# Two-bank PSUM tiles read behind both products, another stage order, and weight sums spread over two chunks, in a fused attention and mixture kernel

## The chip, the cores and the metric

One core of one Trainium2 chip; each call of experiments ran on another chip, with the kernel before beside it. The metric is the device time of one execution in microseconds (us). Each time is a median over repeated executions; profiles show one execution each, and their span is about 2 us shorter than the time of the same run. The interval behind a ratio is its 95% interval.

Engines in the listings: PE does matmuls, PEld loads their weights, DVE is the vector engine, ACT the scalar engine, POOL is GpSimd, SP issues DMAs. PSUM is the memory into which PE writes its products; a tile of it spans two banks in this program, and to evict a result is to read it out of PSUM. The granted clock is PE's clock as the trace records it, 1.00 being full speed. L751 is line 751 of the kernel. In a kernel with another number of lines the same statement may have another number; where it matters, it is said.

## The reference, cut to what matters

```python
# attention over sorted blocks: 4 batches x 8 heads x 768 tokens x 64
P = sinkhorn(sort_net)                       # 8x8 mixing matrices, five rounds
k_sorted, v_sorted = P mixed with k, v       # per head, over 8 blocks of 96 tokens
attn = softmax(scale * q_b @ k_sorted_b.T);  x = attn @ v_sorted_b
# mixture of four experts on the 3072 x 512 result
p = domain_probs / domain_probs.sum(-1)
for e in range(4):
    h = maximum(x @ w1[e], 0)                # w1: 512 x 1024
    out += p[:, e:e+1] * (h @ w2[e])         # w2: 1024 x 512
```

## The kernel before

Everything runs in one program with a hand-made order. The 3072 tokens are worked on in twelve chunks of 256, three to a batch (in the text chunks count from 1, in the code `c` counts from 0). A chunk has hidden-layer groups (16 matmuls each, evicted by DVE in L772) and then second-layer products by a scheme with seven products and sums of operands. The first six chunks (batches 0 and 1) also carry, in numbered slots between their groups and products, the pieces of the next batch's attention: `st_n` and `st_q` load and transpose queries, `st_k` and `st_v` mix keys and values, `st_s` are scores, `st_a` attention, `st_x` the transposed result. The last six chunks use the seven-product scheme on both layers; the change does not touch them.

The slots and who calls them:

```python
def slot(b=b, c=c, at=at):
    here = (c, at[0])                        # chunk, number of the slot
    for cc, n, f, *args in PLANS[b]:         # attention of the next batches
        if (cc, n) == here: f(*args)
    if b:
        for cc, n, e, m in PLAN_A:           # sums of w1 blocks, on DVE, L961
            if (cc, n) == here: input_sums(e, m)
    ...                                      # cut
    at[0] += 1
```

The products of a chunk of batch 0 (c > 0); four banks in two PSUM tiles:

```python
two = [psm([P, 2, 512], F32, ...) for n in range(2)]
bankA, bankB, bankC, bankQ = [two[n // 2][:, n % 2, 0:DH] for n in range(4)]
...                                          # cut
times(bankA, blk(0, 0), "b11", es)           # 12 matmuls of 256 columns (L751)
tt(oa1, bankA, oa1, ALU.add)                 # L855, DVE reads bank A
slot()
times(bankB, blk(1, 0), "b21", es)           # the other bank of the same tile
tt(oa1, bankB, oa1, ALU.add)                 # L858
slot()
...                                          # cut: bank C, bank Q
times(bankA, sm(1), "t2", es, False)         # next writer of the first tile
```

In batch 1 the four experts make 16 matmuls, and instead of L855 ACT copies bank A away (L826) between the two products.

The softmax here doesn't subtract the row's maximum and nothing guards it: scores larger than these inputs give would overflow.

Of the kernel before, what the change touches and what calls it, by code (L numbers as in the profile page):

```python
# [12 lines left out]
ALU = mybir.AluOpType  # L13
# [4 lines left out]
def kernel(  # L18
# [11 lines left out]
    nc = tc.nc  # L30
# [180 lines left out]
    def load_p(b, c):  # L211
        pb = moe.tile([P, E, 2 * P], F32, name=f"pb_{b}_{c}", tag="pb", bufs=1)
        nc.sync.dma_start(
            pb[:],
            p_dram[:, ds(b * S + 2 * c * P, 2 * P)].rearrange("(o e) x -> o e x", o=1).broadcast_to([P, E, 2 * P]),
        )
        return pb
# [380 lines left out]
    def st_bk(b, qd):  # L598
# [4 lines left out]
    PLANS = {  # L603
        0: [
            (0, 9, st_v, 1, 0), (0, 10, st_q, 1, 0), (0, 10, st_v, 1, 1), (0, 11, st_k, 1, 0), (0, 11, st_n, 1, 1),
            (1, 0, st_q, 1, 1), (1, 0, st_k, 1, 1), (1, 0, st_n, 1, 2), (1, 1, st_v, 1, 2), (1, 2, st_s, 1, 0),
            (1, 3, st_v, 1, 3), (1, 3, st_q, 1, 2), (1, 4, st_s, 1, 1), (1, 4, st_n, 1, 3), (1, 5, st_a, 1, 0),
            (1, 6, st_x, 1, 0), (1, 7, st_k, 1, 2), (1, 7, st_lv, 2, 0), (1, 9, st_a, 1, 1), (1, 9, st_q, 1, 3),
            (1, 9, st_lv, 2, 1), (1, 10, st_x, 1, 1),
            (1, 11, st_s, 1, 2), (1, 12, st_lk, 2, 0),  # L610
            (2, 0, st_a, 1, 2), (2, 0, st_n, 2, 0), (2, 0, st_n, 2, 1), (2, 0, st_n, 2, 2), (2, 0, st_n, 2, 3),
# [133 lines left out]
    def times(ps, lhs, rhs, es, first=True, done=True, between=None, at=None):  # L745

        for e in es:
            if e == at:
                between()
            for f in range(KH):  # L750
                nc.tensor.matmul(  # L751
                    ps, lhs(e, f), Ts[e][rhs][:, f, :],
                    start=(first and e == es[0] and f == 0), stop=(done and e == es[-1] and f == KH - 1),
                    skip_group_check=True,
                )
# [25 lines left out]
    def chunk(b, c, slot, done=()):  # L781

        es = list(range(E)) if b else list(range(1, E))
        todo = [e for e in es if e not in done]
        chunk_first(b, c, todo, todo[0], slot)

        for w in range(1, 4 if b else 1 + c if c else 3):
            h_sums(E - 1, w)
        nxt = (b, c + 1) if c + 1 < R // 2 else (b + 1, 0)
        pbs[nxt] = load_p(*nxt)  # L790

        blk = lambda kh, tok: (lambda e, f: Hb[:, e, kh * KH + f, ds(tok * P, P)])
        sm = lambda n: (lambda e, f: Sb[:, n, e, ds(f * P, P)])

        def product(n, lhs, rhs, pool=psm):
            ps = pool([P, DH], F32, f"ps_{n}_{b}_{c}")
            for e in es:
                if pool is last_bank and e == 2:
                    last["e0"][6]()
                for f in range(KH):  # L800
                    nc.tensor.matmul(
                        ps[:], lhs(e, f), Ts[e][rhs][:, f, :],
                        start=(e == es[0] and f == 0), stop=(e == E - 1 and f == KH - 1),
                    )
            return ps[:]

        if b:
            oa, ob = [moeo.tile([P, Dm], F32, name=f"{n}_{b}_{c}", tag="oacc") for n in ("oa", "ob")]
        else:
            oa, ob = oaccs[2 * c], oaccs[2 * c + 1]  # L810
        p1, p5, u2, u3 = [moe.tile([P, DH], F32, name=f"{n}_{b}_{c}", tag=n, bufs=1) for n in ("p1", "p5", "u2", "u3")]
        tt, gtt = nc.vector.tensor_tensor, nc.gpsimd.tensor_tensor
        o = out[ds(b * S, S), :].rearrange("(t p) d -> p t d", p=P)
        oa1, oa2, ob1, ob2 = oa[:, 0:DH], oa[:, DH:Dm], ob[:, 0:DH], ob[:, DH:Dm]

        def store(n, tile):
            nc.sync.dma_start(o[:, 2 * c + n, :], tile[:])

        if b or c:
            two = [psm([P, 2, 512], F32, f"ps_p{n}_{b}_{c}") for n in range(2)]  # L820
            bankA, bankB, bankC, bankQ = [two[n // 2][:, n % 2, 0:DH] for n in range(4)]
            if last:
                bankQ = last["Q"][1][:, 0:DH]
        if b:
            times(bankA, blk(0, 0), "b11", es)
            nc.scalar.copy(p1[:], bankA)  # L826
            slot()
            times(bankB, blk(1, 0), "b21", es)
            tt(oa1, bankB, p1[:], ALU.add)
            slot()  # L830
            times(bankQ, sm(0), "t1", es)
            nc.scalar.copy(p5[:], bankQ)
            slot()
            for e in es:
                h_sums(e, 4)
            times(bankA, sm(1), "t2", es, False)
            nc.scalar.copy(u2[:], bankA)
            slot()
            times(bankC, blk(1, 1), "n4", es)
            nc.scalar.copy(ob1, bankC)  # L840
            slot()
            times(bankA, sm(2), "t3", es, False)
            tt(ob2, bankA, p5[:], ALU.add)
            tt(ob1, bankA, ob1, ALU.add)
            store(1, ob)
            slot()
            times(bankQ, sm(3), "b22", es, False, True, last["e0"][6] if last else None, 2 if last else None)
            tt(oa2, bankQ, u2[:], ALU.add)
            slot()
            store(0, oa)  # L850
            return
        if c:
            both = ob.rearrange("p (h d) -> p h d", h=2)
            times(bankA, blk(0, 0), "b11", es)
            tt(oa1, bankA, oa1, ALU.add)  # L855
            slot()
            times(bankB, blk(1, 0), "b21", es)
            tt(oa1, bankB, oa1, ALU.add)  # L858
            slot()
            for w in range(1 + c, 4):  # L860
                h_sums(E - 1, w)
            times(bankC, blk(1, 1), "n4", es[:1], True, False)
            times(bankQ, sm(0), "t1", es)
            tt(ob2, bankQ, ob2, ALU.add)
            slot()
            for e in es:
                h_sums(e, 4)
            times(bankA, sm(1), "t2", es, False)
            tt(oa2, bankA, oa2, ALU.add)
            slot()  # L870
            next(sums0)
            times(bankC, blk(1, 1), "n4", es[1:], False)
            tt(ob1, bankC, ob1, ALU.add)
            slot()
            times(bankA, sm(2), "t3", es, False)
            tt(both, bankA.rearrange("p (o d) -> p o d", o=1).broadcast_to([P, 2, DH]), both, ALU.add)
            slot()
            store(1, ob)
            next(sums0)
            times(bankQ, sm(3), "b22", es, False)  # L880
            tt(oa2, bankQ, oa2, ALU.add)
            slot()
            store(0, oa)
            return

        def f1():
            nc.scalar.copy(p1[:], product("p1", blk(0, 0), "b11", psm if c == 1 else psa))
            slot()
            gtt(oa1, oa1, p1[:], ALU.add)

        def f2():
            tt(oa1, product("p2", blk(1, 0), "b21"), oa1, ALU.add)
            slot()

        def f3():
            tt(oa2, product("p3", sm(3), "b22"), oa2, ALU.add)
            slot()

        def f4():
            tt(ob1, product("p4", blk(1, 1), "n4"), ob1, ALU.add)  # L900
            slot()

        def f5():
            nc.scalar.copy(p5[:], product("p5", sm(0), "t1"))
            slot()
            gtt(oa2, oa2, p5[:], ALU.add)
            gtt(ob2, ob2, p5[:], ALU.add)

        def last_adds(u3):
            gtt(ob2, u3, ob2, ALU.add)  # L910
            tt(ob1, ob1, u3, ALU.add)

        steps = weight_sums(E - 1, nc.vector)
        f1()
        for e in todo:
            h_sums(e, 4)
        next(steps)
        f2()
        next(steps)
        h_sums(E - 1, 3)  # L920
        f3()
        next(steps)
        f5()
        next(steps)
        tt(u3[:], product("p7", sm(2), "t3"), p1[:], ALU.add)
        slot()
        ps6 = product("p6", sm(1), "t2")
        tt(u2[:], ps6, p1[:], ALU.add)
        tt(u3[:], ps6, u3[:], ALU.add)
        slot()  # L930
        gtt(oa2, u2[:], oa2, ALU.add)
        store(0, oa)
        last_adds(u3[:])
        f4()
        store(1, ob)
# [145 lines left out]
    def last_chunk(g):  # L1081
# [85 lines left out]


    PLAN_A = [
        (1, 11, 0, 0), (1, 13, 0, 1), (2, 1, 0, 2), (2, 2, 1, 0), (2, 3, 1, 1), (2, 4, 1, 2), (2, 5, 2, 0),  # L1170
        (2, 8, 0, 3), (2, 9, 2, 1), (2, 9, 1, 3), (2, 10, 2, 2), (2, 11, 2, 3), (2, 13, 3, 0), (2, 13, 3, 1),
    ]
    late_sums = {(G0, 1): [(3, 2)], (G0, 2): [(3, 3)]}

# [164 lines left out]
```

## Time and profile before

| | before |
|---|---|
| time, median of 3 runs | 382.05 us (381.69 to 382.42) |
| span of the profiled run | 379.1 us |
| PE busy | 358.8 us, 95% |
| PE idle, named after the reads of bank A (L855, L826) | 6.3 us in four waits |
| PE idle, before scores | 3.0 us in two larger waits |
| the last section, six chunks on both layers | 156.5 us from its first product (222.57 us), untouched |

How to read it: PE is the bound nearly throughout, so one looks at what ends each of its idle times, and at whether it runs at full clock. The busy share cannot tell the second: a matmul at half clock counts as busy for longer. The prediction below shows the waits and chains. Four rows of PE's timeline carry one thing more (start, us, engine, line, operation, count, idle before and who ended it), from the third chunk of batch 0:

```profile
116.48 1.92 PE L751 MATMUL ps_p<-w,Hb 128*128 128x256 f16 x12 [2.46 <-DVE room L855]
118.19 1.09 PE L438 MATMUL ps_a<-vs,ET 96*128 96x65 f16 x16
119.09 1.04 PE L751 MATMUL ps_p<-T,Hb 128*128 128x256 f16 x4
119.93 1.89 PE L751 MATMUL ps_p<-w,Sb 128*128 128x256 f16 x12
```

Twelve matmuls of 256 columns take 1.47 us in such a row at full clock, and the 16 of attention 0.65. Behind the 2.46 us wait all four rows are stretched: this is the half clock. In the trace it lasts 3.41 us, from about 117.36 us, so it sets in 0.9 us after PE has resumed.

### The profile page before, as it was taken

To read this page: it belongs to the slowest core of one execution; us is meant where nothing else is said; L and a number is where in the kernel's file an instruction comes from. 1 tells how busy PE (TensorE), PEld (TensorE's weight loads), DVE (VectorE), ACT (ScalarE), POOL (GpSimd) and SP (SyncE) were. 2 spreads that over 40 slices of the span, in tenths; PEclk is the share of its full clock that TensorE was granted. 3 is DMA by queue.
4 is the path that set the end of the run, shared out by engine and by line. 5 is a ranking of instruction groups with operands and counts; after the bars stand their busy time and mean duration, and the time that the engine had idled before them with its cause. 6 is when DMAs were issued, how large, how long until landed. Compare 5 with 4: busy or idle time off the path is not lost.

```text
span 379.1 us, 10548 instructions
## 1 busy us (share of the span) xinstructions
PE 358.8 (95%) x4517; PEld 315.1 (83%) x4517; DVE 280.5 (74%) x558; ACT 157.6 (42%) x282; POOL 117.4 (31%) x134
## 2 busy tenths in 40 slices
PE   8699999967997999999999899999999999999996
PEld 8585858856886887878887799899899898998995
DVE  5654798655896677578669969967868679688694
ACT  2674330533130563436530027347165283471750
POOL 8862101931300054000000005508137064081360
PEclk9999999999998999999999999999999999999999
DMA  8999999999954899963941110220210202103101
GB/s 106 208 208 229 208 209 199 183 177 168 208 70 77 141 164 177 110 124 80 119 105 23 56 43 18 42 73 2 58 57 4 87 26 57 58 2 57 57 13 44
DMA packets 69753, 38.34 MB, mean 101 GB/s; under 512 B 40390, under 2 KB 64716, under 8 KB 69708
## 3 DMA queue, kind: packets, MB, share of 16 engines
q0 software_dynamic: 34640, 17.83, 36.6%
q1 hardware_dynamic: 35068, 19.85, 26.1%
q8 instruction: 35, 0.57, 0.6%
q14 instruction: 10, 0.08, 0.1%
HBM read 42.00 MB, written 6.34 MB: 128 GB/s over the span
## 4 chain that ended last, share of the span: by engine, by line
PE 72%; DVE 14%; DMA 7%; ACT 2%; issue 2%; POOL 2%; DVEq 0%; ACTq 0%; POOLq 0%
PE ps_Q L1114 14%; PE ps_p L751 13%; PE ps_h L766 12%; PE ps_X L1025 8%; PE ps_Q L1025 5%; PE ps_Z L1025 5%; DVE Sb L737 4%; DVE Hb L772 3%; DMA arena<-in_v_dram 3%; PE ps_h L659 3%; PE ps_o L694 3%; DMA qT<-arena 2%; DVE Sb L739 2%; DMA arena<-in_q_dram 2%; PE ps_s L406 1%
## 5 line engine op out<-in xcount | busy, mean ns | idle before, releaser
L1038 POOL TENSOR_TENSOR Hb<-tmp,pb 128x512 f16<-128x512 f32 x48 | 61.9, 1295 | 155.4 <-ACT tmp L1037 153.3
L766 PE MATMUL ps_h<-xT,w 128*128 128x256 f16 x672 | 79.3, 273 | 0.9 <-DVE Hb L772 0.7
L766 PEld LDWEIGHTS <-w 128*128 128x128 f16 x672 | 64.4, 98 | 10.4 <-issue 1.6
L772 DVE SCALAR_TENSOR_TENSOR Hb<-ps_h,pb 128x1024 f16<-128x1024 f32 x42 | 51.3, 1221 | 20.9 <-PE ps_h L766 20.8
L1025 PEld LDWEIGHTS <-w 128*128 128x128 f16 x768 | 46.6, 98 | 1.0 <-issue 0.3
L1114 PEld LDWEIGHTS <-Sb 128*128 128x128 f16 x384 | 36.7, 98 | 6.7 <-DVE Sb L737 2.7
L1025 PEld LDWEIGHTS <-arena 128*128 128x128 f16 x576 | 34.7, 98 | 0.2
L1037 ACT ACTIVATE tmp<-tmp 128x512 f32<-128x512 f32 x48 | 30.5, 635 | 6.4 <-DVE tmp L1069 5.2
L396 ACT CAST kT<-ps_k 64x384 f16<-64x384 f32 x48 | 22.7, 473 | 20.8 <-PE ps_k L387 19.8
L751 PEld LDWEIGHTS <-Sb 128*128 128x128 f16 x288 | 27.7, 99 | 3.8
L1114 PEld LDWEIGHTS <-Hb 128*128 128x128 f16 x288 | 27.4, 98 | 2.9
L751 PEld LDWEIGHTS <-Hb 128*128 128x128 f16 x216 | 20.9, 99 | 10.4 <-issue 7.8
L1025 PE MATMUL ps_X<-kT,arena 128*128 128x128 f16 x384 | 29.3, 219 | 0.0
L121 POOL DMA_DIRECT2D arena<-in_q_dram x24 | 19.8, 837 | 23.6 <-DMA qT<-arena 13.4
L1114 PE MATMUL ps_Q<-w,Sb 128*128 128x256 f16 x192 | 25.8, 273 | 1.0 <-DVE Sb L737 1.0
L737 DVE TENSOR_TENSOR Sb<-Hb 128x512 f16<-128x512 f16 x45 | 26.4, 606 | 0.0
L1061 DVE TENSOR_TENSOR tmp<-ps_Q,tmp 128x512 f32<-128x512 f32 x24 | 16.6, 690 | 12.7 <-ACT tmp L1060 8.5
L413 ACT ACTIVATE ET<-ps_s 96x768 f16<-96x768 f32 x24 | 18.0, 802 | 16.1 <-PE ps_s L406 15.9
L751 PE MATMUL ps_p<-w,Hb 128*128 128x256 f16 x144 | 17.8, 277 | 6.7 <-DVE room L855 5.0
L1114 PE MATMUL ps_Q<-w,Hb 128*128 128x256 f16 x192 | 23.9, 273 | 0.0
L1045 ACT COPY ps_X<-ps_Z 128x512 f32<-128x512 f32 x24 | 13.7, 570 | 23.3 <-PE ps_Z L1025 22.7
L1114 PE MATMUL ps_Q<-T,Sb 128*128 128x256 f16 x192 | 22.9, 273 | 0.0
(188 smaller groups left out, 605.6 us busy)
## 6 DMA issues: line engine op xcount, KB each, us to landing
w<-in_moe_w_dram POOLq DMA_DIRECT2D x7, 1024.0 KB, 27.7
pb<-p_dram SPq DMA_DIRECT2D x12, 512.0 KB, 5.8
arena<-in_k_dram POOLq DMA_DIRECT2D x8, 384.0 KB, 7.9
arena<-in_v_dram POOLq DMA_DIRECT2D x8, 384.0 KB, 9.1
vs<-arena SPq DMA_DIRECT2D x36, 66.0 KB, 5.2
arena<-in_q_dram POOLq DMA_DIRECT2D x24, 96.0 KB, 7.4
out_dram<-ob SPq DMA_DIRECT2D x9, 256.0 KB, 2.0
out_dram<-oa SPq DMA_DIRECT2D x8, 256.0 KB, 2.5
```

The lines of the kernel that those rows point to most:

```text
L121: nc.gpsimd.dma_start(t[:, h // 2, :, h % 2, :], q[b, h].rearrange("(t p) d -> p t d", p=P))
L396: nc.scalar.copy(kT[ds(D * hh, D), r], pk[ds(D * r, D), hh].rearrange("p a (i c) -> p a i c", c=CP),)
L413: nc.scalar.activation(ETs[2 * (pr % 2) + hh][:, 0:S].rearrange("c (a x) -> c a x", a=2), pss[hh][0:BLK, :, 0:HS], AF.Exp, bias=0.0, scale ...
L737: tt(sm[0], blk(0, 1), blk(1, 1), ALU.add)
L751: nc.tensor.matmul(ps, lhs(e, f), Ts[e][rhs][:, f, :], start=(first and e == es[0] and f == 0), stop=(done and e == es[-1] and f == KH - 1 ...
L766: nc.tensor.matmul(ps[:, f, :], w1sb[e][:, kc, ds((4 * g + f) * P, P)], xT[:, kc, ds(2 * c * P, 2 * P)], start=(kc == 0), stop=(kc == NKC ...
L772: nc.vector.scalar_tensor_tensor(out=Hb[:, e, ds(4 * g, 4), :], in0=ps[:], scalar=0.0, op0=ALU.max, in1=pb[:, ds(e, 1), :].broadcast_to([P ...
L1025: nc.tensor.matmul(dst[:, ds(f * P, P)], a[lhs][:, k, ds(f * P, P)], t[rhs][:, k, :], start=(first and f == 0 and k == 0), stop=(f == KH - ...
L1037: nc.scalar.activation(src, src, AF.Relu, bias=0.0, scale=1.0)
L1038: nc.gpsimd.tensor_tensor(Hb[:, e, ds(i * KH, KH), ds(j * P, P)], src.rearrange("p (f x) -> p f x", f=KH), pb[:, ds(e, 1), ds(j * P, P)].b ...
L1061: tt(t22, Q, u3, ALU.add)
L1114: nc.tensor.matmul(ps, lhs(e, f), Ts[e][rhs][:, f, :], start=(first and e == 0 and f == 0), stop=(e == E - 1 and f == KH - 1), skip_group_ ...
```

## The change

Its intent: take PE's idle time out of the chunks of batches 0 and 1. It has three parts and adds or removes no arithmetic.

```diff
-  (1,0,st_n,1,2), (1,1,st_v,1,2), (1,2,st_s,1,0), (1,3,st_v,1,3), (1,3,st_q,1,2), (1,4,st_s,1,1), (1,4,st_n,1,3),
-  (1,5,st_a,1,0), (1,6,st_x,1,0), (1,7,st_k,1,2), ...
+  (1,0,st_n,1,2), (1,1,st_s,1,0), (1,2,st_v,1,2), (1,3,st_v,1,3), (1,3,st_q,1,2), (1,3,st_n,1,3), (1,5,st_s,1,1),
+  (1,6,st_a,1,0), (1,7,st_k,1,2), (1,7,st_x,1,0), ...
@@ products of batch 1
             times(bankA, blk(0, 0), "b11", es)
-            nc.scalar.copy(p1[:], bankA)
             slot()
             times(bankB, blk(1, 0), "b21", es)
+            nc.scalar.copy(p1[:], bankA)
             tt(oa1, bankB, p1[:], ALU.add)
@@ products of batch 0
             times(bankA, blk(0, 0), "b11", es)
-            tt(oa1, bankA, oa1, ALU.add)
             slot()
             times(bankB, blk(1, 0), "b21", es)
+            tt(oa1, bankA, oa1, ALU.add)
             tt(oa1, bankB, oa1, ALU.add)
@@ weight sums: (chunk, slot, expert, sum)
-  (1,11,0,0), (1,13,0,1), (2,1,0,2), (2,2,1,0), (2,3,1,1), (2,4,1,2), (2,5,2,0), (2,8,0,3), (2,9,2,1), ...
+  (1,8,0,0), (1,10,0,1), (1,12,0,2), (1,12,1,0), (1,13,1,1), (1,14,1,2), (2,2,2,0), (2,4,2,1), (2,6,2,2), (2,9,0,3), ...
```

## The prediction

> **What bounds the kernel now.** I read the busy shares first, then the tensor engine's waits, then the chain of work that ended last around each wait, and last the timelines of PE, DVE and ACT there.
>
> From the page (engine, busy us, share of the span; then the granted clock in 40 slices of 9.5 us):
>
> ```profile
> PE 358.8 (95%) x4517; PEld 315.1 (83%) x4517; DVE 280.5 (74%) x558; ACT 157.6 (42%) x282; POOL 117.4 (31%) x134
> ...
> PEclk9999999999998999999999999999999999999999
> ```
>
> PE is busy nearly throughout, so only what removes PE's idle time, or PE time at a lower clock, can pay; the change removes no matmul. One slice (114 to 123 us) has a lower clock: the clock record in the trace has a stretch of 3.41 us at half speed from about 116.5 us.
>
> The waits of PE that the change can touch (engine, output, line <- releaser: total us, times, longest):
>
> ```profile
> PE ps_p L751 <- DVE room L855: 5.0, 2, 2.5
> ...
> PE ps_s L406 <- DMA qT<-arena: 1.6, 1, 1.6
> ...
> PE ps_s L406 <- ACT arena L360: 1.4, 1, 1.4
> ...
> PE ps_p L751 <- ACT p L826: 1.3, 2, 0.8
> ```
>
> L855 and L826 read bank A, the first half of a two-bank PSUM tile; the matmuls that wait for them write bank B, the other half. The kernel has five such places (second and third chunk of batch 0, three chunks of batch 1), and in all five B starts only after A's read ends. Nothing in the data asks for that: the wait comes with sharing the tile.
>
> The chain around the first place (start, us, what):
>
> ```profile
> 69.35 6.28 DMA arena<-in_q_dram
> 75.63 0.02 issue
> 75.64 8.92 DMA qT<-arena
> 84.57 0.05 issue
> 84.61 0.51 PE ps_s L406 x16
> 85.13 1.87 PE ps_h L766 x16
> ...
> 87.02 1.23 DVE Hb L772
> ...
> 89.06 0.69 DVE xsl L423
> ...
> 89.89 0.69 DVE xsl L423
> 90.58 0.33 DVE Sb L737
> 90.91 0.34 DVE room L855
> 91.26 0.04 issue
> 91.30 1.47 PE ps_p L751 x12
> ```
>
> The scores of batch 1's second head pair wait for transposed queries, which land at 84.57. After them comes one more group of hidden-layer matmuls (1.75 us), and then B's product stands behind everything DVE has queued ahead of the read of A: the last group's eviction, two normalisations of attention, a sum.
>
> Third, the last chunk of batch 1:
>
> ```profile
> 207.75 1.21 DVE Hb L772
> 208.96 0.33 DVE Sb L739
> 209.29 0.34 DVE Sb L741
> 209.63 0.60 DVE arena L961
> 210.23 1.15 DVE Hb L772
> 211.38 0.04 issue
> 211.42 1.92 PE ps_p L751 x16
> ```
>
> Here DVE sets the pace (17.29 of the 18 us from 194 to 212 are DVE-busy): evictions L772 at about 1.13 us start to start, sums of activations at 0.33, and the weight sums L961 at 0.60 each stand in one queue, and PE's next product waits for the eviction that ends it.
>
> **What the Trainium skill says.** "PSUM — Partial Sum Buffer", section "PSUM bank collisions raise a hardware error", asks for guarding PSUM by bank and quadrant. The trace is stricter: two different banks of one tile are ordered, five times of five. "TensorE: Matmul & The Clock Gate", Part 1, describes a clock halved by an idle activity window of 3413 ns that runs free; the trace agrees in length (3.41 us at 0.5, at a PE wait of 2.46 us), but the wait of 2.52 us at 88.8 brought no such stretch, so the phase matters. "DMA: Bandwidth & Descriptors", "Issuing engines are not separate DMA queues", has all DMAs share 16 engines: the trace agrees, the transpose took 8.9 us from issue at 75.6 and 2.7 us when issued near 122, where the DMAs were less busy. "Perfetto Trace Analysis", "Optimization Strategy", advises judging each regime by itself, as I do.
>
> **The change part by part.** The pieces of attention are called at numbered slots: after each group of hidden-layer matmuls, then after each product. One 128x256 product over three experts is 12 matmuls, 1.31 us start to end of stream; over four experts 16, 1.75 us; an attention product 0.48; scores 0.44; a v or k stage 0.33.
>
> *Other stage order (chunk 2 of batch 0).* The first scores move ahead of the v stage whose ACT cast (L360) waits for earlier stores of v. I follow PE from 72.7: first group to 74.79; scores, half of them held until ACT finishes evicting the k stage at 75.17, so done about 75.65; four more groups and two v stages, then the sixth group ends near 83.3. The second scores now stand after all six groups. But their queries still land at 84.57: those loads and the transpose are issued ahead of all that moves, and the software DMA queue is full either way. So PE waits 1.2 us, scores 84.61 to 85.06, and the former sixth group (1.75 us) is already done. What replaces the old 1.45 and 1.57 us waits is one wait that ends at the same moment; the gain is the group moved in front of it.
>
> *Banks read behind both products, same chunk.* Product A 85.06 to 86.37; attention, with its second half held about 0.05 to 0.1 us until ACT's exponentials end (85.1 + 2x0.75), to 86.9; B at 86.9 in place of 91.30: 4.4 us gained. Now the order behind it: DVE normalises until about 88.4, then reads A and B until 89.1. The next writer of that tile is the t2 product, after a k stage and 16 matmuls, at 90.25, so the delayed reads are hidden. Later the last product waits about 0.3 us for DVE's read of bank C. I keep 4.25 at the chunk's end.
>
> *Same, chunk 3 of batch 0.* A ends at 113.87 and B started at 116.48: 2.6 us. Without this idle time the half-speed stretch should go too: B's 12 matmuls took 1.75 instead of 1.31, attention 0.88 instead of 0.48, the next four 0.84 instead of 0.44, together 1.2 us. Following the rest of the chunk with DVE's queue (reads of A and B at 116.02 to 116.7, normalisation to 118.4, then 0.34 to 0.7 per instruction) gives two new waits of about 0.1 and 0.15 us, and the chunk ends at 123.46 on the old clock of the trace against 127.44: 4.0 us. The last transposed input, issued at 118.45 with 2.8 us to landing (as the one issued at 120.7 has now), is there by 121.3, before 123.46.
>
> *Batch 1, chunks 1 and 2.* In the first, A ends 145.93 and B started 146.84 because ACT's copy stood behind four casts of k: 0.9 us; but the scores two stages on need a buffer that DVE's normalisation frees, which comes only about 0.5 us earlier: 0.65 us kept. In the second, B starts 0.3 us earlier and ACT's copy moves behind the casts, which frees another buffer 0.35 us earlier: 0.35 kept.
>
> *Weight sums over two chunks, and chunk 3 of batch 1.* Six weight sums instead of two lie in chunk 2, where DVE has gaps of 1.7, 1.1, 2.3 and 0.9 us; three fit into them whole, the one in its last slot delays the first eviction of chunk 3 by about 0.4 us, eating the 0.35. Then only two sums instead of five stand ahead of the seventh eviction: 3x0.60 = 1.8 us less on DVE, so it ends at 209.65 instead of 211.36. PE's eight groups, followed against these evictions, end at 209.65 too. A starts at 209.9 (211.42 before), and B follows at once at 211.65 (213.84 before, of which 0.67 was the wait for the copy): 2.2 us. DVE's queue behind it has room, since two sums fewer stand after A as well; I expect the 2.2 to last to the start of the last section (about 153 us, from 227), which the change does not alter.
>
> Sum: 4.25 + 4.0 + 0.65 + 2.2 = 11.1 us. I take off 0.9 for waits I cannot see, mostly the transposed queries of the third head pair: issued about 84.65 with 9.2 us to landing, as now, they arrive at 93.9, and PE wants them at 94.2. 382.05 - 10.2 = 371.8 us.
>
> **The rivals.** (1) *The data is the bound around 100 us.* DMA is at 90% or more until about 104 us, so work moved earlier may only wait for queries or transposed inputs. For: the second scores do exactly this. Against: the third pair's queries had 3 us to spare before (landed 95.5, used 98.76), and their transpose moves forward by 1.6 us. If half the first gain is lost: 374. (2) *DVE takes PE's place.* The reads queue up behind the normalisations and the tile is then late for t2. For: in chunk 3 of batch 0 DVE is 0.75 us behind. Against: 1.75 us of other products lie in between. If t2 waits a microsecond in each of five chunks: 376, within 2%. (3) *ACT's copy now waits for B too*, so DVE's sum of both is late and drags the normalisations. That is already in the 0.65; double it and 0.5 us more is lost. (4) *The half-speed stretch moves and does not go*, since its window runs free: the new 1.2 us wait is shorter than any that brought one, but if so, 1.2 us is lost: 373. (5) Better than expected: if the queries land earlier than 84.57, up to 1.2 us more.
>
> **Range and chances.** Each of the two large terms is tied to starts and ends in the trace to some tenths; downstream waits are likelier to take than to give. 80% range: 369.0 to 375.5. The 2% line is 374.4, so the gain must fall by a quarter to miss it: faster 0.86, within 2% 0.13, slower 0.01.
>
> **What would show it.** The wait of L751 for L855 and for L826 gone; scores of the second pair still released by the query transpose near 84.6, with an idle of about 1.2 us; B about 87; chunk 3 of batch 0 starting its products near 108 and no half-speed stretch there; the last section starting about 10 to 11 us earlier and lasting as long as now. Wrong would be: a wait of L751 for the new reads of A and B ahead of t2, a wait of the third pair's scores for queries of over 1 us, or a DVE-paced last chunk of batch 1 as long as before.

## The result, and the profile after

| | before | after |
|---|---|---|
| time, median, same rounds | 381.87 us (380.89 to 382.42, 4 runs) | 370.75 us (370.15 to 371.02, 4 runs) |
| ratio, 95% interval | | 0.971 (0.969 to 0.973) |
| span of the profiled run | 379.1 us | 368.1 us |

The change is faster by 2.9%. The prediction was 371.8 us.

The page of the changed kernel, busy shares and clock:

```profile
PE 356.6 (97%) x4517; PEld 314.3 (85%) x4517; DVE 280.3 (76%) x558; ACT 157.6 (43%) x282; POOL 117.4 (32%) x134
...
PEclk9999999999999999999999999999999999999999
```

The same matmuls are 2.2 us less busy. Most of it is the slice with the lower clock, which is gone: the first experiment's kernel, with no such slice and the same matmuls, shows 357.2 us.

The chain around the second scores (start, us, what), to be held against the one of before in the prediction:

```profile
75.51 8.76 DMA qT<-arena
84.32 0.51 PE ps_s L406 x16
84.84 1.42 PE ps_p L751 x12
86.25 0.57 PE ps_a L438 x16
86.83 1.31 PE ps_p L751 x12
```

The queries still end PE's wait at 84.3 us. But the next piece is product A and not the last hidden group, and product B follows the attention at once: it starts at 86.7 us in the timeline, where it started at 91.30.

The third chunk of batch 0 (PE's timeline):

```profile
107.93 2.78 PE L751 MATMUL ps_p<-w,Hb 128*128 128x256 f16 x24
110.55 0.65 PE L438 MATMUL ps_a<-vs,ET 96*128 96x65 f16 x16
111.03 0.60 PE L751 MATMUL ps_p<-T,Hb 128*128 128x256 f16 x4
```

A and B are one unbroken row of 24 matmuls, and the attention is back at 0.65 us.

Where the 11.0 us between the two spans lie, by the start of each part in PE's two timelines:

| part | before us | after us | shorter by |
|---|---|---|---|
| start to the hidden groups of chunk 2, batch 0 | 70.96 | 70.26 | 0.70 |
| chunk 2, batch 0 | 29.65 | 25.72 | 3.93 |
| chunk 3, batch 0, hidden groups | 11.95 | 11.95 | 0 |
| chunk 3, batch 0, products | 14.88 | 11.01 | 3.87 |
| chunk 1, batch 1, hidden groups | 16.74 | 16.73 | 0.01 |
| chunk 1, batch 1, products | 16.21 | 15.64 | 0.57 |
| chunk 2, batch 1, hidden groups | 18.29 | 18.29 | 0 |
| chunk 2, batch 1, products | 16.04 | 16.03 | 0.01 |
| chunk 3, batch 1, hidden groups | 16.70 | 15.45 | 1.25 |
| chunk 3, batch 1, to the last section's first product | 11.15 | 10.48 | 0.67 |
| the rest | 156.5 | 156.5 | 0 |

The first row is no effect of the change, which begins later: it is how the first loads fell in these two executions. It does not come on top in full, either. The changed kernel reached chunk 2 of batch 0 earlier by 0.70, but its queries landed only about 0.3 earlier, so part of it went into that wait. The second row counts that part as a loss. Counted from the start of the second scores (84.61 and 84.32), the gain of chunk 2 is 4.63 - 0.29 = 4.34 us.

### The profile page after: what moved, and what is told of

Same layout as the page of the kernel before. It is cut to its first block, busy times and chain, and to the rows that moved or that the text cites. A ratio compares the mean times of both kernels' runs of the same rounds, so it can differ in the third digit from the quotient of the medians.

```text
span 368.1 us, 10549 instructions
## 1 busy us (share of the span) xinstructions
PE 356.6 (97%) x4517; PEld 314.3 (85%) x4517; DVE 280.3 (76%) x558; ACT 157.6 (43%) x282; POOL 117.4 (32%) x134
## 4 chain that ended last, share of the span: by engine, by line
PE 73%; DVE 12%; DMA 7%; ACT 3%; issue 2%; POOL 2%; DVEq 0%; ACTq 0%; POOLq 0%
PE ps_Q L1114 15%; PE ps_h L766 14%; PE ps_p L751 11%; PE ps_X L1025 8%; PE ps_Q L1025 6%; PE ps_Z L1025 5%; DVE Sb L737 4%; PE ps_h L659 3%; DMA arena<-in_v_dram 3%; PE ps_o L694 3%; DMA qT<-arena 2%; DMA arena<-in_q_dram 2%; DVE Sb L739 2%; ACT kT L396 2%; DVE xsl L423 2%
## 5 line engine op out<-in xcount | busy, mean ns | idle before, releaser
L772 DVE SCALAR_TENSOR_TENSOR Hb<-ps_h,pb 128x1024 f16<-128x1024 f32 x42 | 51.2, 1222 | 17.1 <-PE ps_h L766 17.1
L1052 ACT COPY tmp<-ps_X 128x512 f32<-128x512 f32 x24 | 14.1, 587 | 12.2 <-PE ps_X L1025 12.2
```

What stands on the lines that cost most here:

```text
L772: nc.vector.scalar_tensor_tensor(out=Hb[:, e, ds(4 * g, 4), :], in0=ps[:], scalar=0.0, op0=ALU.max, in1=pb[:, ds(e, 1), :].broadcast_to([P ...
```

## The experiments

Eleven kernels ran, all correct; the kernel before ran 11 times beside each call. Diffs are against the kernel before, or against the changed one where it says so.

**The three parts alone.** First the stage order: the `PLANS` part of the diff above and nothing else.

> Only the other stage order in the second chunk of batch 0; banks and weight sums as before. Theory: the gain of this chunk comes from getting the sixth hidden group in front of the wait for the queries and from DVE having no normalisation queued ahead of its read of bank A (the attention now stands behind that read). So the read of A runs while PE does the attention, bank B's product waits under 0.2 us though the banks still share a tile, and the chunk gains 4.2 to 4.4 us: time 0.988 to 0.990 of before. The second wait of 2.5 us (third chunk of batch 0) stays. Rival, parts that simply add: the order is worth only the group of 1.75 us, the 2.5 us wait for the read of A stays in the second chunk too: 0.995.

Measured: 375.91 us, ratio 0.986 (0.982 to 0.990), a little more than expected. PE's timeline:

```profile
84.62 0.52 PE L406 MATMUL ps_s<-qT,kT 64*128 64x96 f16 x16 [1.08 <-DMA qT<-arena]
85.06 1.48 PE L751 MATMUL ps_p<-w,Hb 128*128 128x256 f16 x12
86.38 0.73 PE L438 MATMUL ps_a<-vs,ET 96*128 96x65 f16 x16
87.06 1.47 PE L751 MATMUL ps_p<-w,Hb 128*128 128x256 f16 x12
```

Bank B starts at 87.06, with the read of A still in front of it: DVE was idle when A ended, so it read A (from 86.58) during the attention. Chunk 2 took 25.33 us (29.65 before). The parts do not simply add: in this chunk the stage order alone brings nearly all that the whole change brings. Note that the second 2.5 us wait stayed, yet chunk 3's products took 13.26 us and not 14.88. The 1.62 us between them are the half clock, which this execution did not have; the fourth experiment starts there.

The reads of banks alone (the two hunks of products):

> Only the reads of banks A and B behind both products, in all five places; stage order and weight sums as before. Theory: 2.5 us in the second chunk of batch 0, 3.9 in the third (of which about 1.2 from the half-speed clock that goes), 0.55 in the first chunk of batch 1, 0 in the second, 0.6 in the third: 7.5 us, time 0.980 to 0.982 of before. No wait of L751 for a read of A. Rival (the delayed reads come too late for the t2 product, which waits in their place): under 5 us, 0.987 or more, with a wait of L751 for DVE ahead of t2.

Measured: 373.58 us, ratio 0.979 (0.976 to 0.982), so as expected and a little more. In chunk 2, A and B are one row, and the t2 product follows without a wait:

```profile
87.12 2.79 PE L751 MATMUL ps_p<-w,Hb 128*128 128x256 f16 x24
...
91.82 1.47 PE L751 MATMUL ps_p<-T,Sb 128*128 128x256 f16 x12
```

The products of chunk 2 took 10.69 us (13.31 before), those of chunk 3 11.01. No product waits for a read of A, and none waits for DVE ahead of the t2 product. The later reads are hidden.

The weight sums alone (the `PLAN_A` hunk):

> Only the weight sums spread over two chunks. Theory: the last chunk of batch 1 is paced by DVE in its hidden groups, three sums less stand ahead of the seventh eviction, one delays the first: 1.2 to 1.5 us gained there and nowhere else, time 0.996 to 0.997 of before, both waits of 2.5 us untouched. Rival (DVE is not the pace-setter there, or the moved sums delay the chunk before as much): 0.999 to 1.001.

Measured: 381.01 us, ratio 0.997 (0.994 to 1.001). The ratio is the expected one, but its interval holds 1, so by time this is inconclusive. In the trace the hidden groups of batch 1's chunk 3 took 15.44 us against 16.70 in the kernel before, 15.45 in the changed one, and the chunks before it show no loss. That agrees with 1.26 us gained; it is read from one execution.

**Does the idle time bring the half clock, and at what price?** Forty matmuls that nobody reads, in the wait of chunk 3:

```diff
             tt(oa1, bankA, oa1, ALU.add)
+            if c == 2:
+                ps_warm = psa([P, 2, 512], F32, "ps_warm")
+                for _ in range(40):
+                    nc.tensor.matmul(ps_warm[:, 0, 0:P], ident[:], ident[:], start=True, stop=True)
             slot()
```

> The kernel before with 40 matmuls of 128 columns on the identity matrix, into a PSUM tile that nobody reads, put between products A and B in the third chunk of batch 0: PE still waits until about 116.4 us for the read of A, but is busy during it. Theory: the half-speed stretch at 116.5 us comes of PE's idle time there and cost about 1.2 us; with PE busy it is gone, and the time falls by 1.0 to 1.4 us: 0.9965 of before, the wait itself (L855) shrinking to under 0.6 us in the listing without being worth anything. Rival (the low clock has another cause, or its cost is hidden by the later waits): 0.999 to 1.001.

Measured: 381.51 us, ratio 1.000 (0.996 to 1.004). By its time my expectation fell. The trace tells why:

```profile
91.36 1.53 PE L751 MATMUL ps_p<-w,Hb 128*128 128x256 f16 x12 [2.52 <-DVE room L855]
...
94.17 2.40 PE L751 MATMUL ps_p<-w,Sb 128*128 128x256 f16 x12
```

The stretch was gone from chunk 3 (13.26 us) and stood in chunk 2, whose products took 14.96 instead of 13.31 us. So a stretch can follow either wait, and which executions get it differs: the profiled kernel before had one stretch, the profile of the weight sums alone had one in each of the two waits and one near the start.

So the next kernel kept PE busy in both waits (28 such matmuls in chunk 2, 40 in chunk 3, same edit without the `if`):

> The kernel before with matmuls on the identity, into a PSUM tile that nobody reads, in both of its 2.5 us waits (28 in the second chunk of batch 0, as far as a free buffer lets them start early, 40 in the third). Both waits for the read of bank A stay, PE is busy in most of them. Theory now: each 2.5 us idle can bring a half-speed stretch of 3.4 us, which costs 1.65 us, and an execution draws none, one or two of them; so with PE busy no stretch is left in the products of batch 0 and every run should look like the fastest of before: about 379.5 to 380.2 us, ratio 0.993 to 0.997, with a narrower spread. Rival (the spread of before has another source, or the stretch moves elsewhere): ratio 0.999 to 1.001 and the same spread.

Measured: 380.17 us (379.54 to 380.33), ratio 0.995 (0.993 to 0.998), beside 380.76 to 383.08 of the kernel before. It keeps both waits and removes no work, and is faster and steadier. The listed runs carry each execution's mean clock too. Of the 33 runs of the kernel before that stand beside these experiments, the one at clock 1.000 took 379.42 us; twelve at 0.995 or 0.996 took 380.74 to 381.90; eighteen at 0.991 took 380.72 to 383.42; two at 0.987 took 383.5. One stretch of 3.41 us at half speed lowers the mean over 379 us by 0.0045, so by this count these are none, one, two and three stretches. The changed kernel's runs stand at 0.998 to 1.000. Not every stretch costs the same: this kernel still had one from about 17 us in its trace, in the preparations, and its runs at clock 0.994 or 0.995 took 379.56 to 380.33 us, those at 0.999 or 1.000 took 379.54 and 380.17.

Two things in the traces go beyond this. In the four stretches behind the waits (the kernel before, the fourth experiment, two in the weight sums alone) the clock fell only 0.2 to 1.3 us after PE had resumed, so the price is paid by the work behind the wait. And the stretch at 17 us followed no long wait: in the 3.41 us before it PE was busy for 2.34 us, and its longest listed wait was 0.48 us. So the length of one wait does not settle whether the clock falls; what does is not shown here.

**Is the wait one of the tile?** The kernel before, with banks B and C swapped in batch 0, so that A and B lie in different tiles:

```diff
             bankA, bankB, bankC, bankQ = [two[n // 2][:, n % 2, 0:DH] for n in range(4)]
+            if not b:
+                bankB, bankC = bankC, bankB
```

> The kernel before with bank B moved to the other PSUM tile (banks B and C swapped) in the second and third chunk of batch 0; reads of A and B stay where they were. Theory (the wait is an order kept per tile, not per bank): product B starts right at A's end in both chunks, under 0.2 us, and the first product that shares A's new tile (bank C, four matmuls) waits for the read of A in its place, about 1.0 us in the second chunk and 0.8 in the third; the gain is 1.7 + 1.8 us and the half-speed stretch, 0.986 to 0.991 of before. Rival (the wait is for DVE itself or for the bank, whatever the tile): B still waits 2.5 us, 0.999 to 1.001.

Measured: 379.09 us, ratio 0.994 (0.992 to 0.996), short of what I expected. PE's timeline in chunk 2 (the two lines added move L855 to L857 and L873 to L875, the reads of A and C):

```profile
87.19 2.79 PE L751 MATMUL ps_p<-w,Hb 128*128 128x256 f16 x24
...
91.19 0.60 PE L751 MATMUL ps_p<-T,Hb 128*128 128x256 f16 x4 [0.87 <-DVE room L857]
...
97.64 1.47 PE L751 MATMUL ps_p<-T,Sb 128*128 128x256 f16 x12 [1.57 <-DVE room L875]
```

The theory of the tile held: B runs on from A at once. In chunk 3 it waited 0.66 us, which the listing puts down to the eviction L772 of the tile's former content, and not for the read of A. The gain did not come. Bank C now waits for the read of A, and later the t3 product into A waits 1.57 us for the read of C, its new neighbour. Chunk 2's products took 13.62 us, longer than the 13.31 of before; chunk 3's 12.63 against 13.26 without a stretch. The two chunks together are only 0.3 us shorter than without a stretch (26.25 us in place of 26.57), so most of the 0.6% is likely the clock: these runs stand at 0.995 to 1.000. Moving a bank moves the wait; moving the reads behind both products removes it.

**The largest wait that the change left: the queries.** Against the changed kernel, the second pair's loads and transpose are called earlier:

```diff
-  (0,9,st_v,1,0), ..., (0,11,st_n,1,1), (1,0,st_q,1,1), ...
+  (0,8,st_n,1,1), (0,9,st_v,1,0), ..., (0,11,st_q,1,1), ...
```

> The changed kernel with the loads of the second head pair's queries of batch 1 called at the ninth slot of the first chunk instead of the twelfth, ahead of two GpSimd adds, and their transpose ahead of two stores. Theory: the end of the wait at the second scores (1.56 us, the largest that the change left) is set by this chain alone; the transpose is issued about 3 us earlier, PE finds the queries there, and 1.0 to 1.6 us are gained on the changed kernel: 0.966 to 0.969 of before. Rival (the data of the whole stretch to 100 us are bandwidth-bound, so the wait moves to the third pair's scores): no gain, 0.970 to 0.972.

Measured: 370.27 us, ratio 0.969 (0.967 to 0.972), not told apart from the changed kernel. The second scores no longer waited, but the third did:

```profile
94.45 0.52 PE L406 MATMUL ps_s<-qT,kT 64*128 64x96 f16 x16 [1.33 <-DVE room L876]
```

The outcome is the rival's: the wait moved to the third pair. The listing names a DVE add, L876. It had begun at 93.6 and ended just before; but the third pair's transpose, issued at 85.09 with 9.2 us to landing, came in at 94.3 as well. A last experiment in this row separates the two: the third transpose one slot earlier, ahead of the six stores of v in SP's queue (`(1,3,st_q,1,2)` becomes `(1,2,st_q,1,2)` and stands before `st_v`).

> The changed kernel with the query chain of the second head pair called early, as in the kernel that tried only that, and the third pair's transpose called one slot earlier, ahead of the six stores of v in SyncE's queue. There the wait at the second scores went but 1.33 us came back at the third scores, named after a DVE add, while the third transpose (issued 85.1, 9.2 us to landing) landed at 94.3, just as those scores started. Theory: that transpose was the cause; issued near 78 it lands before 90, and the third scores do not wait: 1.2 to 1.6 us gained on the changed kernel, 0.9660 to 0.9680 of before. Rival (DVE's add L876 is what holds the third scores, as the listing says): the 1.3 us stay there, 0.969 to 0.971.

Measured: 369.03 us, ratio 0.9645 (0.962 to 0.967). The transpose was issued at 77.23 with 6.5 us to landing, and

```profile
93.04 0.52 PE L406 MATMUL ps_s<-qT,kT 64*128 64x96 f16 x16
```

has no wait. So it was the transpose, not the DVE add that the listing named. The traces say the same of the add: in this run it began at 93.63 and in the changed kernel at 94.72, each time after the third scores had started (93.04 and 94.13). Nor was it bandwidth alone, as the rival had it, since no transfer was taken out: when the transpose was issued decided. The gain is somewhat more than expected.

**Why chunk 2 of batch 1 gained nothing.** The changed kernel again, with half of the casts of k of two head pairs on DVE:

```diff
-                nc.scalar.copy(
+                (nc.vector.tensor_copy if hh and b == 3 and pr > 1 else nc.scalar.copy)(
```

> The changed kernel with half of the casts of k of batch 3's last two head pairs on DVE instead of ACT. Theory: in the second chunk of batch 1 the earlier product B gained nothing because the attention behind it waits for a PSUM buffer that ACT's four casts of k hold until 173.9 us (its 16 matmuls took 0.93 instead of 0.65 us in the listing, twice); with two casts on DVE the buffer is free a microsecond earlier and both attention products take 0.65: this chunk is 0.5 to 0.9 us shorter, 0.9685 to 0.9700 of before. Rival (DVE's normalisations, pushed back by the casts, hold the next buffers): chunk as long as in the changed kernel, 0.9709.

Measured: 373.17 us, ratio 0.978 (0.976 to 0.980): slower than the changed kernel, not faster. PE, then DVE:

```profile
175.47 0.40 PE L438 MATMUL ps_a<-vs,ET 96*128 96x65 f16 x8 [0.38 <-DVE kT L396]
...
183.25 0.21 PE L406 MATMUL ps_s<-qT,kT 64*128 64x96 f16 x1 [0.78 <-DVE xsl L423]
```

```profile
174.19 1.13 DVE L396 CAST kT<-ps_k 64x384 f16<-64x384 f32 x2 [0.67 <-ACT kT L396]
```

The attention does wait for the casts of k, as said; that wait is now named after DVE. But DVE's two casts started only when ACT's two had ended, so nothing ran side by side, and DVE's normalisations came later and held up the scores behind. The products of this chunk took 18.23 us in place of 16.03. Whether the shared input tile or the shared output tile puts the casts in a row, these runs do not tell.

**A better version.** The kernel with both query chains early, and one build of a mixing matrix on DVE (L327) moved into a gap of DVE: `(1,1,st_bk,3,0)` becomes `(0,12,st_bk,3,0)` in batch 1's plan.

> The same, and the build of one PI matrix on DVE (L327, 0.68 us) moved from the hidden groups of the second chunk of batch 1 to a gap of DVE among the products of the first. Theory: in the changed kernel PE waits 0.41 us for it, and the scores behind 0.22 us more; both go: another 0.4 to 0.7 us, 0.9645 to 0.9668 of before. Rival (the chunk is paced by the evictions there, or the build delays the normalisations before it): same as without the move.

Measured: 368.38 us (367.71 to 368.94), ratio 0.963 (0.961 to 0.966). The wait of 0.41 us for L327 is gone, and the gain is again a little above what was expected.

> The changed kernel itself, on the chip and in the rounds of the two variants, to compare with. 0.969 to 0.972 of before, spread under 1.5 us, no half-speed stretch in the products of batch 0.

Measured: 370.34 us (370.31 to 370.51, five runs), ratio 0.9685 (0.966 to 0.971), from the same rounds. Against it the two variants are 1.3 and 2.0 us faster by their medians, without overlap of their runs with its own. The second is the fastest of all kernels here by median; its runs and those of the first variant overlap, so that the moved build pays is likely and not shown beyond doubt.

## Why the prediction was right

**Other stage order.** Right in mechanism and size. PE still waited for the queries until their transpose landed, and the sixth group stood in front of it (84.32 us, 1.56 us idle; I said 84.61 and 1.2, the difference being the earlier start of this execution). Counted from the scores, product B came 4.35 us earlier (2.34 us behind them in place of 6.69) and the chunk's end 4.34; I said 4.4 and kept 4.25; the stage order alone gave 4.32 in its trace. The prediction added this part and the banks in one chain and so did not say that in this chunk either one makes most of the other unnecessary: 4.3 and 2.6 us alone, 4.3 together.

**Banks behind both products.** The wait for the read of A is gone in all five places, and the later reads do not delay t2. Chunk 3 of batch 0 gave 3.87 us (4.0 predicted). The printed terms do not make that 4.0: 2.6 for the wait and 1.2 for the clock, less 0.25 for two new waits, are 3.55. The 4.0 came from following PE to 123.46, and this holds more clock than the three rows that I listed, since a fourth row, at 119.93, was stretched too. So the half clock was the mis-sized term: it costs 1.62 to 1.65 us (14.88 against 13.26 in chunk 3, 14.96 against 13.31 in chunk 2). The rest is 2.25 us, the wait less two new ones of about 0.23 and 0.14 us.

**Batch 1, chunks 1 and 2.** Chunk 1: 0.57 us for 0.65, with the scores held by DVE's normalisation as predicted. Chunk 2: 0.01 for 0.35. This step failed: "In the second, B starts 0.3 us earlier and ACT's copy moves behind the casts, which frees another buffer 0.35 us earlier: 0.35 kept." The casts did not start earlier. Their k stage runs in the slot between A and B, at the same point as before, and the attention behind the earlier B waits for their end. PE's rows show the wait inside one row, as a long duration, and ACT's show what it waits for:

```profile
171.69 1.91 PE L751 MATMUL ps_p<-w,Hb 128*128 128x256 f16 x16
173.44 0.93 PE L438 MATMUL ps_a<-vs,ET 96*128 96x65 f16 x16
```

```profile
171.95 1.97 ACT L396 CAST kT<-ps_k 64x384 f16<-64x384 f32 x4 [0.74 <-PE ps_k L387]
```

The casts end at 173.92, and the attention, 0.65 us elsewhere, ends late.

**Weight sums, and chunk 3 of batch 1.** Predicted 2.2 us together with the 0.35 above, measured 1.25 in the hidden groups and 0.67 at the copy, 1.92. The difference, 0.28, is about the 0.35 that chunk 2 did not hand on.

**The 0.9 us taken off** for unseen waits were not needed. The third pair's transpose, which I named, was issued at 84.11 and landed 7.7 us later, over two microseconds before its use. Without this discount the sum of 11.1 us would have given 370.95, beside 370.75 measured. That it comes so near is in part luck: 0.29 us of the 11.0 between the traces is the earlier start, so the parts that the change touched make 10.7, and the runs of the kernel before alone span 1.5 us.

**Slips that changed nothing.** The half clock begins at about 117.36 us and not at 116.5; from 227 us to the end of the span it is 152 us and not 153; and in the second rival 371.8 and 5 us make 376.8, not 376.

**What I had not seen** is that the kernel before has no single time: its runs carry up to three stretches of half clock, and its profiled run happened to carry one in the part concerned. With none on either side the two kernels are about 379.4 (one run) and 370.3 us, 9.1 us apart; by this estimate the rest of the 11.1 us is clock that the changed kernel no longer loses.

## What to carry to other kernels

When two products go to the two banks of one PSUM tile, read both banks behind both products, if nothing needs the first early; and see whether the reads then still come before the tile's next writer. Before adding up the parts of a change, ask of each whether another part already takes away what it waits for. When a microsecond is to be explained, list the granted clock of each run beside its time, because an idle time of 2.5 us may cost its own length and, in some executions, 1.65 us more.

## What the Trainium skill lacked or had wrong

- "Perfetto Trace Analysis", section "Optimizing Tensor Performance", Matmuls, advises rotating independent matmul groups through different PSUM banks so that the eviction of one overlaps the matmuls of the next. It lacks that two banks inside one tile did not overlap: product B waited for the read of A in five of five places, up to 2.5 us, and in chunk 2 ran on at once when A and B were in different tiles.
- "PSUM — Partial Sum Buffer", section "PSUM bank collisions raise a hardware error", asks for guarding by bank and quadrant. The waits in this program were kept per tile, which is stricter; no page says what that costs (2.25 us in one chunk here, without the clock).
- "TensorE: Matmul & The Clock Gate", section "HAM oscillation — how this bites in real kernels", gives the rule of no PE idle gap above about 3.4 us. Here shorter gaps were followed by half speed: behind waits of 2.5 us a stretch of 3.41 us came in some executions and not in others, at 1.62 to 1.65 us each, and two profiled executions had one near 17 us with no listed wait above 0.52 us in the 3.4 us before it. A wait of 2.02 us (near 78 us, fourth experiment) brought none. The half speed itself agrees with the page.
- "DMA: Bandwidth & Descriptors", section "DMA Transpose (X-bar)", gives no time to landing beside other traffic: transposes of queries, alike in size, took from 2.7 us (few other DMAs) to 9.2 us (beside loads on the software queue), and their landing ended two waits here.
- No page warns that the releaser named by a listing may be a coincidence: the 1.33 us "DVE room L876" went away when a transpose was issued earlier.
